# A linear-attention and mixture-of-experts kernel on one core: all steps put in another order by a planner with other prices for changes of the array's tiling

## The chip, the cores and the metric

The kernel runs on one core of one Trainium2 chip. The metric is the device time of one execution in microseconds, as the median of three runs. Engines are named as the profile names them: PE is TensorE (PEld its weight loads), DVE is VectorE, ACT is ScalarE, POOL is GpSimd, SP is the engine that issues most DMAs.

## What is computed

For 8 batches and 8 heads (sequence 576, head size 64), linear attention with a feature map, and then on its output a layer with 4 experts, each a causal softmax attention of its own, mixed by a gate that keeps the two best experts of a row:

```python
def phi(x):
    proj = np.einsum('bhsd,df->bhsf', x, w_phi)
    proj = proj - np.max(np.abs(proj), axis=-1, keepdims=True)
    return np.concatenate([np.exp(proj), np.exp(-proj)], axis=-1)
kv = np.einsum('bhsf,bhsd->bhfd', k_p, v)
num = np.einsum('bhsf,bhfd->bhsd', q_p, kv)
den = np.einsum('bhsf,bhf->bhs', q_p, z)[..., None] + 1e-06
x = num / den                          # per batch: 576 x 512
for e in range(4):
    q, k, v = x @ wq[e], x @ wk[e], x @ wv[e]
    a = softmax(causal(scale * q @ k.T))
    ye = a @ v @ wo[e]
    out += weight_of_gate(x @ w_gate, e) * ye
```

## The kernel before

Work is cut into steps. A pair is two heads of the first part (32 pairs in all, 4 to a batch); a half of a batch is two experts (16 halves in all). The steps on PE, with the line of the profile and the part of the 128x128 array that a matmul takes:

- **full array** (128 rows, 128 columns): L315, the helper `mm`, serves the projections of x to q and k (`ps_c<-xh,qk`), to v and the gate (`ps_c<-vg,xh`, five tiles a batch, called V steps here), the output projection (`ps_c<-yh,wo`, eight units a batch), and short warming matmuls on the tile `warm` that fill PE's waits at the start. L633 transposes.
- **64 rows**: L509, the feature projections of K and Q of a pair (`k_in`, `q_in` with `wf`), and L838, the scores, in four banks for each half.
- **32 columns**: L605 and L622 (kv and its sums of keys), L710 (denominators), L721 (numerators), L924 (gates), L1001 (the sums of the softmax), L1030 (attention times v).

So PE goes back and forth between three tilings of the array. A change of tiling is a point in PE's order where the next matmul takes another part of the array than the last.

All results land in eight PSUM tiles (`ps_c`), taken from one pool. A tile is free again when ACT or DVE has copied or used up what it holds: the two halves of Q's projection wait for copies on ACT (`evac_u`, L324), K's for DVE (`center`, L564 and L578), the denominators' and the softmax sums' for a chain DVE, ACT, DVE (`fractions`, L732, L326, L739, L742, L745) at the end of which the tile is released, the scores' for copies on ACT (`evac_s`).

After the scores of a half come the mask on POOL (L942), the running maximum over key blocks (`top`, L955, DVE), the maximum across partitions on POOL (L959, into the tile `max`), subtraction (L963, DVE), exponential (L326, ACT), two additions into `max` (L975, DVE), and the sums (L1001, PE). There is one `max` tile, so the L959 of a half has to wait until the L1001 of the half before has read it.

No order is written out by hand. Each stream of steps is a generator; the class `Plan` keeps an estimated clock for each engine, and at each turn looks for the steps that could start within `WINDOW` of the earliest and takes the one with the lowest position. Positions come from the tables `POS`, `POS1`, `BOFF` and `MOVE` (one number for each step), plus `OTHER` where a step would change the tiling; `SWITCH` is added to the start of such a step. What a matmul costs in the estimate stands in `mm`, `half_mm` and `scores`, and what a change costs in `run`:

```python
        if eng == 'PE' and tiling != self.tiling:
            cost += CHANGE[tiling == (128, 128)]
            self.tiling = tiling
```

with `CHANGE = (150.0, 190.0)`: 150 ns into 64 rows or 32 columns, 190 ns into the full array. The order in which the steps are taken is then fixed on each engine by `in_order`.

Of the kernel before, what the change touches and what calls it, by code (L numbers as in the profile page):

```python
# [16 lines left out]
B, H, S, D, F = 8, 8, 576, 64, 128  # L17
# [23 lines left out]
HOT = 22.62  # L41
SLOPE = (-27.1, -45.11, 31.37, 22.04, 0.2)
# [5 lines left out]
FLEX = (544, -30)  # L48
# [6 lines left out]
WINDOW = 53.0  # L55
SWITCH = 43.0
SLACK = 150.0
LATE = (1200.0, 500.0)
PHASE = 0.0
ZEROS = 34.47  # L60

MOVE = {
# [10 lines left out]
    'evu': (21.12, -4.06, 14.36, -18.44, 5.1, 15.91, 29.23, -7.85, 16.87, -12.86, 9.23, -24.49, -1.82, -0.22, -20.76, 24.81, 11.28, -7.35, 2.92, 2.45, 9.93, -6.72, -3.41, -34.68, -21.04, 1.48, -2.83, 22.44, -22.76, -6.25, 15.97, -11.69,),  # L73
    'ph0': (-8.14, 0.95, 0.11, -1.26, 2.32, -7.14, 14.26, 1.03, -4.68, 5.71, 17.28, -2.71, 7.54, -8.69, 8.12, 18.24, -7.03, 16.87, -6.18, -9.54, -25.96, 24.71, -7.89, 12.56, -1.56, 10.54, -2, -6.36, -29.4, -8.19, -24.29, 4.42,),
    'ph1': (0.98, -31.26, 7.61, 13.17, -13.03, -6.78, -4.19, 30.31, 1.24, 14.84, -16.58, -8.83, -2.18, 2.26, -24.69, 4.64, 4.19, -14.28, -5.42, 5.41, 8.16, -8.76, -6.61, 2.72, -6.37, 21.76, -7.17, -16.16, -0.85, 16.73, 11.84, -11.68,),
    'cen': (-18.81, 6.49, -10.84, 12.73, -20.02, 8.22, 2.67, -4.13, -37.26, -31.66, -22.98, -21.09, -1.99, 11.55, -10.57, 24.02, 3.96, -3.59, 2.44, 14.24, 5.39, 33.73, 12.84, 2.35, -5.61, -5.03, -22.36, 21.58, -8.41, -5.42, -15.78, 16.67,),
    'evd': (-0.53, -8.66, 7.47, -22, -18.99, -9.4, -18.15, 12.47, -19.84, 8.28, -2.9, -3.62, 17.77, 27.72, -5.5, -22.57, 11.69, -3.3, -11.95, -21.43, -1.49, 34.49, 13.92, 18.59, 3.14, 4.37, 4.81, 2.48, 26.02, 6.28, 12.39, -10.59,),
    'n1': (7.63, -9.91, 2.94, 8.61, 6.97, 3.71, 0.17, -10.61, -19.77, -1.78, -4.43, -30.48, -18.43, 0.14, 9.45, -11.23, -16.35, -18.78, 7.28, 10.47, 7.42, -28.12, 5.4, 14, -24.35, -5.88, -12.01, -7.61, 17.16, -5.33, -22.39, -11.91,),
    'div': (-24.16, 1.89, 13.29, 2.53, 0.65, -0.28, 8.21, -7.67, -3.37, 4.47, -12.51, 7.23, 1.58, -6.78, 5.93, 2.54, 10.1, -14.14, -5.17, -6.51, 26.08, -8.09, -24.63, 7.57, 4.12, 2.66, -35.81, -1.48, 11.92, -19.86, -16.37, -36.85,),
# [1077 lines left out]
```

## Time and profile before

| what | value |
|---|---|
| median of three runs | 617.29 us (616.87 to 617.4) |
| span of the profiled execution | 615.0 us |
| PE busy | 600.5 us, 98% of the span |
| DVE busy | 557.3 us, 91% |
| ACT busy | 432.0 us, 70% |
| POOL busy | 245.0 us, 40% |
| granted TensorE clock, mean | 0.997 |
| chain that ended last, by engine | PE 74%, DVE 15%, ACT 5%, DMA 2%, issue 2% |

The span runs from the first to the last instruction of the profiled execution, whose own time beyond its span was not recorded apart; the median lies 2.3 us above the span. Matmuls are pipelined and the ends of their rows are modelled, so a PE row's length is longer than the time until the next matmul starts, and a short wait of PE can lie under the row before it. In the chain of waits a PE piece is cut where the next begins, so its length is the time that the group took on the path.

### The profile page before, as it was taken

The numbers are of one execution on the slowest core, as the hardware profiler recorded it, in microseconds if no ns is written. First come the engines' busy times: TensorE is split into PE (matmuls) and PEld (weight loads), VectorE is DVE, ScalarE is ACT, GpSimd is POOL, SyncE is SP. The second block draws the span as 40 slices with busy tenths as digits, with TensorE's granted clock in tenths as the row PEclk, the third lists the DMA queues.
The fourth block names the chain that finished last, engine by engine and source line by source line (L and its number), as shares of the span: only waits on it lengthen the run. The fifth ranks groups of instructions, "written<-read, shape, count | busy, mean of one in ns | idle before, by whom it ended". The sixth has DMA issues, their size and how long they took to land.

```text
span 615.0 us, 19992 instructions
## 1 busy us (share of the span) xinstructions
PE 600.5 (98%) x8263; PEld 470.6 (77%) x8263; DVE 557.3 (91%) x1124; ACT 432.0 (70%) x1034; POOL 245.0 (40%) x167
## 2 busy tenths in 40 slices
PE   8999999999999999999999999999999999999987
PEld 7665788667796778768886868876889677878976
DVE  5899989999999999999899999999999998888793
ACT  4898786667687688677775885875796668556652
POOL 5635533453324644252333614418430706421420
PEclk9999999999999999999999999999999999999999
DMA  9553212253113431253214332144212311020022
GB/s 218 155 150 103 59 51 81 68 159 87 54 66 113 120 87 37 72 158 110 74 35 107 119 107 63 46 135 138 66 53 83 111 37 27 15 92 2 2 78 78
DMA packets 41610, 52.48 MB, mean 85 GB/s; under 512 B 21168, under 2 KB 24624, under 8 KB 41520
## 3 DMA queue, kind: packets, MB, share of 16 engines
q1 hardware_dynamic: 41200, 50.62, 28.5%
q8 instruction: 65, 1.06, 0.7%
q10 hardware_dynamic: 320, 0.59, 0.4%
q14 instruction: 25, 0.20, 0.1%
HBM read 36.64 MB, written 14.55 MB: 83 GB/s over the span
## 4 chain that ended last, share of the span: by engine, by line
PE 74%; DVE 15%; ACT 5%; DMA 2%; issue 2%; POOLq 1%; POOL 1%; SPq 0%; ACTq 0%; DVEq 0%
PE ps_c L315 29%; PE ps_c L509 9%; PE ps_c L605 9%; PE ps_c L721 7%; PE ps_c L1030 6%; PE ps_c L838 6%; PE ps_c L710 4%; DVE u L685 3%; DVE zs L546 2%; PE ps_c L622 2%; ACT ek L326 2%; PE ps_c L1001 1%; DVE s L963 1%; DVE ek L578 1%; DVE max L975 1%
## 5 line engine op out<-in xcount | busy, mean ns | idle before, releaser
L681 POOL PARTITION_ALL_REDUCE mx<-u x64 | 144.2, 2305 | 182.7 <-ACT u L324 165.9
L315 PE MATMUL ps_c<-xh,qk 128*128 128x320 f32 (+1 forms) x512 | 106.1, 298 | 0.0
L959 POOL PARTITION_ALL_REDUCE max<-top x16 | 59.9, 3745 | 101.5 <-DVE top L955 35.8
L315 PEld LDWEIGHTS ps_c<-xh,qk 128*128 128x128 f32 x512 | 82.7, 188 | 2.3 <-issue 0.7
L326 ACT ACTIVATE ek<-ek 128x1152 f32<-128x1152 f32 x64 | 75.0, 1171 | 5.7 <-DVE ek L578 5.0
L315 PE MATMUL ps_c<-xl,qk 128*128 128x256 f32 (+1 forms) x256 | 75.5, 295 | 0.0
L605 PE MATMUL ps_c<-ek,v_in 128*32 128x256 f32 x1280 | 75.4, 381 | 0.0
L963 DVE TENSOR_TENSOR s<-s,max 128x1152 f32<-128x1152 f32 (+4 forms) x80 | 68.3, 879 | 1.0 <-POOL max L959 1.0
L942 POOL TENSOR_SCALAR_AFFINE_SELECT s<-s 128x256 f32<-128x256 f32 (+1 forms) x80 | 41.5, 558 | 62.2 <-ACT s L324 61.9
L685 DVE TENSOR_TENSOR u<-u,mx 128x576 f32<-128x576 f32 x64 | 61.6, 975 | 3.9 <-POOL mx L681 3.9
L324 ACT COPY s<-ps_c 128x512 f32<-128x512 f32 (+4 forms) x152 | 52.7, 445 | 14.7 <-PE ps_c L838 14.4
L326 ACT ACTIVATE s<-s 128x1152 f32<-128x1152 f32 (+4 forms) x80 | 56.4, 740 | 8.6 <-DVE s L963 8.4
L605 PEld LDWEIGHTS ps_c<-ek,v_in 128*32 128x32 f32 x1280 | 39.7, 110 | 27.2 <-issue 1.3
L315 PE MATMUL ps_c<-vg,xh 128*128 128x260 f32 (+1 forms) x320 | 58.9, 286 | 0.3 <-ACT s L324 0.3
L564 DVE TENSOR_REDUCE pmax<-ps_c 128x4 f32<-128x512 f32 (+1 forms) x96 | 49.5, 539 | 8.1 <-PE ps_c L509 8.0
L315 PE MATMUL ps_c<-yh,wo 128*128 128x320 f32 (+1 forms) x256 | 53.1, 303 | 0.0
L326 ACT ACTIVATE mx<-u 128x576 f32<-128x576 f32 x64 | 43.9, 687 | 10.5 <-DVE u L685 10.4
L324 ACT COPY u<-ps_c 128x256 f32<-128x256 f32 (+1 forms) x127 | 41.6, 412 | 11.7 <-PE ps_c L509 11.4
L578 DVE TENSOR_TENSOR ek<-ps_c,pmax 128x512 f32<-128x512 f32 (+1 forms) x96 | 49.8, 537 | 0.0
L315 PEld LDWEIGHTS ps_c<-vg,xh 128*128 128x128 f32 (+1 forms) x320 | 47.4, 177 | 1.9 <-ACT s L324 0.8
L509 PEld LDWEIGHTS ps_c<-wf,k_in 64*128 64x128 f32 x576 | 41.9, 190 | 8.5 <-ACT u L324 3.0
L509 PE MATMUL ps_c<-wf,k_in 64*128 64x128 f32 x576 | 46.7, 283 | 1.5 <-ACT u L324 1.1
(124 smaller groups left out, 1399.4 us busy)
## 6 DMA issues: line engine op xcount, KB each, us to landing
v_in<-in_v_dram SPq DMA_DIRECT2D x32, 320.0 KB, 3.0
out_dram<-ot SPq DMA_DIRECT2D x32, 288.0 KB, 2.1
q_in<-in_qt_dram SPq DMA_DIRECT2D x60, 144.0 KB, 2.9
kvd<-kvt SPq DMA_DIRECT2D x104, 48.0 KB, 1.7
kv<-kvd SPq DMA_DIRECT2D x26, 192.0 KB, 2.6
k_in<-in_kt_dram SPq DMA_DIRECT2D x32, 144.0 KB, 2.8
k_in<-in_kt_dram SPq DMA_DIRECT2D x32, 128.0 KB, 2.8
q_in<-in_qt_dram ACTq DMA_DIRECT2D x4, 144.0 KB, 4.1
```

The lines of the kernel that those rows point to most:

```text
L315: nc.tensor.matmul(o, a, b, start=start, stop=stop, skip_group_check=True)
L324: nc.scalar.copy(o, i)
L326: nc.scalar.activation(o, i, func, **kw)
L509: nc.tensor.matmul(o, a, b, start=True, stop=True, skip_group_check=True)
L564: dve(n * 128, [mk], [pk]).tensor_reduce(out=m[:, us], in_=src, axis=AX.X, op=ALU.max, apply_absolute_value=True)
L578: dve(n * 128, [e1k], [pk, mk]).tensor_tensor(out=ek2[p % EKB][:, 1, us, :], in0=src, in1=m[:, us].unsqueeze(2).to_broadcast([128, n, 128] ...
L605: nc.tensor.matmul(o[g, 0:2], v_in[:, 4 * h + t if t < 4 else 8 + h, k:64:2], ek[:, :, u_, :].rearrange("p c (w f) -> p c w f", w=4), star ...
L681: nc.gpsimd.partition_all_reduce(M, U, 128, bass_isa.ReduceOp.absmax)
L685: (nc.gpsimd if st.eng == 'POOL' else nc.vector).tensor_tensor(out=U, in0=U, in1=M, op=ALU.subtract)
L721: nc.tensor.matmul(ps[g:g + 32, 0:n], kvi[:, 2 * k + h, 32 * c:32 * c + 32], P_[h][c][:, s0:s1], start=c == 0, stop=c == 1, skip_group_che ...
L959: nc.gpsimd.partition_all_reduce(big.rearrange("p e s -> p (e s)"), top.rearrange("p e s -> p (e s)"), 128, bass_isa.ReduceOp.max)
L963: dve(2 * (S - 128 * j), [('d', x, j)], [('max', z)], 1.11, True).tensor_tensor(out=block(s_, j, None, rows(j)), in0=block(s_, j, None, ro ...
```

## The change

Instructions, tiles, buffers and transfers stay. The planner's prices change: each of the six kinds of change of tiling (F full array, R 64 rows, C 32 columns) gets its own, the matmuls of 64 rows get dearer by 3 to 8%, those of the full array a little cheaper, and all numbers of the position tables are new. Of these tables two lines stand here for all:

```diff
-HOT = 22.62
-SLOPE = (-27.1, -45.11, 31.37, 22.04, 0.2)
+HOT = 17.96
+SLOPE = (-111.44, -251.27, 40.23, 60.34, 22.07)
-FLEX = (544, -30)
+FLEX = (544.69, -42.6)
-WINDOW = 53.0
-SWITCH = 43.0
-SLACK = 150.0
-LATE = (1200.0, 500.0)
+WINDOW = 54.35
+SWITCH = 52.31
+SLACK = 165.59
+LATE = (1273.05, 546.05)
...
-    'm1': (7.02, 3.31, 27, -26.54, -1.83, 9.53, -13, -0.23,),
+    'm1': (7.41, 35.39, 147.3, -15.84, -4.59, 231.04, -76.16, -16.72,),
...
-TRATE = 2.37
-CHANGE = (150.0, 190.0)
+TRATE = 2.4
+CHANGE = {'FR': 102.0, 'FC': 110.0, 'RF': 141.0, 'RC': 163.0, 'CF': 116.0, 'CR': 110.0}
-OTHER = 20.47
+OTHER = 26.82
+ROWS = (1.055, 1.083)
...
+def change_cost(a, b):
+    kind = ['C' if t[1] < 128 else 'R' if t[0] < 128 else 'F' for t in (a or (128, 128), b)]
+    return CHANGE.get(''.join(kind), 0.0)
...
-            cost += CHANGE[tiling == (128, 128)]
+            cost += change_cost(self.tiling, tiling)
...
-            cost = max(n / RATE, LDW) + 5
+            cost = max(0.4454 * n, LDW) + 4.3
...
-        plan.run('PE', 2 * alone * n / TRATE + 3, [w], r, tiling=(64, 128))
+        plan.run('PE', alone * ROWS[n == 128] * (2 * n / 2.37 + 3), [w], r, tiling=(64, 128))
```

Lines of the new kernel stand six further down (L509 is L515 there, L1001 is L1007).

Counted in the two orders, PE changes its tiling 169 times before and 212 times after. Stretches of the full array go from 46 to 58, those of 64 rows from 59 to 75, those of 32 columns from 64 to 79 (each counted where it is entered). The warming matmuls go from 117 to 132, all in the first part. On DVE 1126 instructions become 1122, on ACT 1040 become 1044, since each copy may go to either.

Three places. The first is on PE, in the third batch, after the denominators of a pair, its neighbour's kv and sums of keys (L605, L622 with `ek`, `zs`) come Q's projection (L509, two matmuls of 256 and two of 320 columns) and the numerators (L721). Before:

```order
L622 MATMUL ps_c_65<-ek_108,sel 32x4x32 x4
L509 MATMUL ps_c_68<-q_in_105,wf 128x256
L509 MATMUL ps_c_70<-q_in_105,wf 128x256
L509 MATMUL ps_c_64<-q_in_105,wf 128x320
L509 MATMUL ps_c_66<-q_in_105,wf 128x320
L721 MATMUL ps_c_68<-mx_137,kv_119 32x256 x2
L721 MATMUL ps_c_68<-mx_138,kv_119 32x256 x2
L721 MATMUL ps_c_68<-u_129,kv_119 32x256 x2
L721 MATMUL ps_c_68<-u_130,kv_119 32x256 x2
```

After:

```order
L628 MATMUL ps_c_69<-ek_108,sel 32x4x32 x4
L515 MATMUL ps_c_63<-q_in_105,wf 128x256
L515 MATMUL ps_c_64<-q_in_105,wf 128x256
L727 MATMUL ps_c_68<-mx_137,kv_119 32x256 x2
L727 MATMUL ps_c_68<-mx_138,kv_119 32x256 x2
L727 MATMUL ps_c_68<-u_129,kv_119 32x256 x2
L727 MATMUL ps_c_68<-u_130,kv_119 32x256 x2
L515 MATMUL ps_c_69<-q_in_105,wf 128x320
L515 MATMUL ps_c_63<-q_in_105,wf 128x320
```

The halves of Q's projection, which stood in one stretch, now have the first half of the numerators between them: two changes of tiling more. The tile that the numerators take (68) was Q's own a step earlier before, and is another one now.

The second place is on PE near the end, where the last V step (`vg`) is followed by the output projection of the last batch but one (`wo`) and the softmax sums of the last half but one (L1001). Before:

```order
L315 MATMUL ps_c_66<-vg,xl_146 64x260
L315 MATMUL ps_c_68<-yh_167,wo 128x256 x2
L315 MATMUL ps_c_68<-yl_168,wo 128x256
L315 MATMUL ps_c_68<-yh_169,wo 128x256 x2
L315 MATMUL ps_c_68<-yl_170,wo 128x256
L315 MATMUL ps_c_69<-yh_167,wo 128x320 x2
L315 MATMUL ps_c_69<-yl_168,wo 128x320
L315 MATMUL ps_c_69<-yh_169,wo 128x320 x2
L315 MATMUL ps_c_69<-yl_170,wo 128x320
L1001 MATMUL ps_c_70<-s_153,ones 32x64 x4
```

After:

```order
L321 MATMUL ps_c_64<-vg,xl_146 64x260
L1007 MATMUL ps_c_70<-s_153,ones 32x64 x4
L1007 MATMUL ps_c_70<-max_156,ones 32x224 x4
L1007 MATMUL ps_c_70<-s_153,ones 32x96 x4
L1007 MATMUL ps_c_70<-s_153,ones 32x32 x4
L321 MATMUL ps_c_69<-yh_167,wo 128x256 x2
L321 MATMUL ps_c_69<-yl_168,wo 128x256
L321 MATMUL ps_c_69<-yh_169,wo 128x256 x2
L321 MATMUL ps_c_69<-yl_170,wo 128x256
```

The sums stand ahead of the two output units that were ahead of them.

The third place is what these sums wait for, on DVE: the running maximum of the last half (`top`, L955) and the two additions of the half before (L975). Before:

```order
L955 TENSOR_TENSOR top_155<-s_154 128x2x448
L955 TENSOR_TENSOR top_155<-top_155,s_154 128x2x320
L955 TENSOR_TENSOR top_155<-top_155,s_154 128x2x192
L955 TENSOR_TENSOR top_155<-top_155,s_154 64x2x64
L963 TENSOR_TENSOR s_153<-s_153,max_156 64x2x64
L975 TENSOR_TENSOR max_156<-s_153 128x2x448
L975 TENSOR_TENSOR max_156<-max_156,s_153 128x2x320
```

After:

```order
L961 TENSOR_TENSOR top_155<-s_154 128x2x448
L981 TENSOR_TENSOR max_156<-s_153 128x2x448
L961 TENSOR_TENSOR top_155<-top_155,s_154 128x2x320
L981 TENSOR_TENSOR max_156<-max_156,s_153 128x2x320
L961 TENSOR_TENSOR top_155<-top_155,s_154 128x2x192
L961 TENSOR_TENSOR top_155<-top_155,s_154 64x2x64
```

The two additions have one maximum (of 320 columns) between them and two of the four behind them; the last subtraction (L963) went ahead of the whole row.

## Rows read from the trace of the kernel before

**Rows 1.** The page, part 1: busy time, share of the span and instructions of each engine.

```profile
span 615.0 us, 19992 instructions
PE 600.5 (98%) x8263; PEld 470.6 (77%) x8263; DVE 557.3 (91%) x1124; ACT 432.0 (70%) x1034; POOL 245.0 (40%) x167
```

**Rows 2.** Windows: start and end, length, each engine's busy time, clock, DMA.

```profile
50.00:580.00 530.00, 524.68 (x7187) 411.67 (x7184) 494.19 (x985) 375.71 (x913) 215.49 (x146) 1.00 0.27 78
```

**Rows 3.** PE's waits between 50 and 580 us, the longest four of seven: total, times, longest.

```profile
PE ps_c L838 <- DVE rb L745: 1.7, 2, 1.3
PE ps_c L509 <- ACT u L324: 1.1, 2, 0.6
PE ps_c L838 <- DVE xl L319: 1.0, 1, 1.0
PE ps_c L710 <- DMA kv<-kvd: 0.5, 1, 0.5
...
```

**Rows 4.** Chain of waits: start, length, what; 32 columns, after the same tiling and after another.

```profile
112.43 2.20 PE ps_c L605 x39
114.63 2.70 PE ps_c L1030 x56
...
356.56 2.66 PE ps_c L315 x18
359.22 2.84 PE ps_c L1030 x56
```

**Rows 5.** The same view for 64 rows: the 18 matmuls of a K step.

```profile
90.94 2.60 PE ps_c L838 x33
93.54 1.17 PE ps_c L509 x18
...
442.29 6.55 PE ps_c L315 x48
448.84 1.32 PE ps_c L509 x18
```

**Rows 6.** The same view for the full array: one V step alone, between scores.

```profile
313.03 1.63 PE ps_c L315 x12
```

**Rows 7.** Timeline of PE: the first matmuls of two V steps, twelve matmuls apart.

```profile
244.56 0.40 PE L315 MATMUL ps_c<-vg,xh 128*128 128x260 f32 x2
...
245.99 0.40 PE L315 MATMUL ps_c<-vg,xh 128*128 128x260 f32 x2
```

**Rows 8.** Timeline at 219 us: softmax sums, the release of their tile, the scores.

```profile
219.12 0.41 PE L1001 MATMUL ps_c<-s,ones 128*32 128x96 f32 x16
...
225.42 0.77 DVE L745 STREAM_TRANSPOSE rb<-ps_c 128x576 f32<-128x576 f32 x1
...
226.24 0.47 PE L838 MATMUL ps_c<-qh,kkh 64*128 64x448 f32 x1 [1.26 <-DVE rb L745]
```

**Rows 9.** Timeline near the end: maxima, additions, output units, sums, POOL's maximum.

```profile
582.63 1.80 DVE L955 TENSOR_TENSOR top<-top,s 128x640 f32<-128x640 f32 x3
...
584.74 1.09 DVE L975 TENSOR_TENSOR max<-s 128x896 f32<-128x896 f32 x1
...
585.85 0.40 PE L315 MATMUL ps_c<-yh,wo 128*128 128x256 f32 x2
...
585.94 0.82 DVE L975 TENSOR_TENSOR max<-max,s 128x640 f32<-128x640 f32 x1
...
587.54 0.32 PE L1001 MATMUL ps_c<-s,ones 128*32 128x64 f32 x8
...
588.37 3.58 POOL L959 PARTITION_ALL_REDUCE max<-top  x1 [6.72 <-PE ps_c L1001]
```

**Rows 10.** Timeline at the start: warming matmuls, DVE.

```profile
10.04 4.36 PE L315 MATMUL ps_c<-warm 128*128 128x128 bf16 x75
...
14.52 1.85 DVE L685 TENSOR_TENSOR u<-u,mx 128x576 f32<-128x576 f32 x1 [0.26 <-POOL mx L681]
...
16.30 1.27 DVE L564 TENSOR_REDUCE pmax<-ps_c 128x4 f32<-128x512 f32 x2
```

More of the change, by code (lines that the diff above doesn't have):

```diff
@@ L54 @@
 WINDOW_HAM = 3413.0
-WINDOW = 53.0
-SWITCH = 43.0
-SLACK = 150.0
-LATE = (1200.0, 500.0)
+WINDOW = 54.35
+SWITCH = 52.31
+SLACK = 165.59
+LATE = (1273.05, 546.05)
 PHASE = 0.0
-ZEROS = 34.47
+ZEROS = 28.2
 MOVE = {
[10 rows of a table removed]
[L73 to L79, printed above, removed]
[6 rows of a table removed]
-    'gate': (19.49, -11.43, -6.09, 0.85, 5.59, 17.09, 4.34, 6.95,),
-    't1': (6.21, -13.36, 7.09, -2.21, -6.96, -5.15, -13.11, -22.93,),
-    'out': (0.94, -2.47, -1.22, -1.17, -4.2, 1.36, 15.49, 6.05,),
-    'fin': (0, 0, 0, 0, 0, 0, 0, -0.18,),
-}
@@ L91 @@
-POS1 = {'wq': 24.27, 'wv': 48.25, 'wo': 6.32, 'n0': -29.41, 'n1': 1.65, 'k': -1.55, 'q': -17.83, 'v': 6.22, 'kv': -23.07, 'z': 0.35, 'cen': -7.3, 'evu': -37.47, 'ph0': 25.81, 'ph1': 20.93, 'div': 3.92, 'evd': -3.25, 'lk': -12.81, 'lq': 47.36}
-BOFF = (-5.07, 0.34, -2.66, -3.42, -4.38, 5.28, 25.26, 8.75)
-POS = {'fin': 20.11, 'p0': -6.7, 'p1': -66.09, 'v0': 14.93, 'gate': -16.07, 's0': 3.48, 's1': -24.31, 'm0': 14.77, 'm1': 13.89, 't0': -38.13, 't1': 12.5, 'out': 23.34}
[10 rows of a table added]
+    'evu': (208.22, -120.66, -21.82, -22.61, -16.71, -69.18, 165.88, -61.01, 237.38, 146.65, -167.82, -53.3, 248.63, 119.02, -277.18, 43.31, -235.6, -77, -194.35, 70.77, -305.4, 183.89, -3.86, -156.53, 2.84, -46.31, 80.54, 86.55, 16.54, -66.97, 137.96, -198.95,),
@@ new lines @@
+    'ph0': (27.44, 54.88, -96.31, 55.7, -0.74, -6.58, 46.74, -211.33, 112.41, 127.15, 144.36, -18.6, 144.21, -57.98, 337.59, 42.04, 145.16, 14.41, 49.26, -49.85, 81.72, 16.06, -54.75, 172.77, 103.18, -25.71, -128.25, 62.97, 51.69, -187.3, -12.88, -1.58,),
+    'ph1': (51.04, -185.15, 97.8, 311.74, 109.46, -9.8, -4.78, 80.65, 58.22, 151.09, -13.13, -179.25, 185.43, 39.28, -29.47, 95.76, -4.63, 63.95, -173.35, 98.94, -51.32, -22.26, 15.84, -84.66, 87.94, -17.29, 117.6, -39.93, -47.74, 178.93, -75.42, 295.48,),
@@ new lines @@
+    'cen': (89.75, 82.81, -83.16, -142.1, -70.22, 16.7, -65.11, -277.87, -16.42, -39.64, -97.91, -50.3, -103.81, 13.96, -50.77, 68.09, 6.96, 39.64, -82.26, -58.6, -60.54, -28.89, 25.71, -23.34, -212.23, 59.21, -126.89, 5.29, -246.55, -164.39, -59.85, -134.3,),
+    'evd': (-69.52, -188.56, 20.22, 20.85, 39.02, -6.93, -33.01, -46.09, -147.11, 184.47, -151, -106.86, -73.8, 71.54, -237.35, -13.59, -103.54, -31.34, -71.31, 15.7, -53.54, -20.66, 58.35, -23.95, 53.23, 24.85, 41.31, -54.42, 98.26, 118.15, -149.38, -120.33,),
@@ new lines @@
+    'n1': (75.59, -139.79, -149.7, -75.7, 23.15, -72.38, 117.13, 155.26, 15.86, 48.36, 24.57, 145.51, -33.45, -110.33, 28.21, 26.85, -18.75, -37.25, -448.32, -176.75, -25.95, -162.32, 118.17, 114.01, 33.01, -175.75, -75.24, -67.53, 38.17, -33.48, -510.45, 179.74,),
+    'div': (-89.49, -23.11, 60.23, -114.07, 158.85, 25.89, -137.24, -62.44, -304.95, -198.76, -23.11, 8.98, 39.87, -194.04, -258.93, -120.66, -251, -62.07, 14.2, -134.99, 27.84, -66.59, -78.15, -242.74, -52.76, 123.95, 113.22, -310.3, -194.65, 74.68, 12.61, -65.84,),
[6 rows of a table added]
@@ new lines @@
+    'gate': (25.45, -22.5, -40.62, -19.86, -55.33, -9.16, 4.09, -168.81,),
+    't1': (-53.98, -31.39, -136.77, 58.41, 19.35, 27.37, 166.59, -151.07,),
+    'out': (24.21, -15.56, -28.63, -23.3, 256.67, 354.4, -64.07, 135.51,),
+    'fin': (0, 0, 0, 0, 0, 0, 0, -66.52,),
+}
+POS1 = {'wq': 59.63, 'wv': 73.23, 'wo': 38.56, 'n0': -38.06, 'n1': -2.97, 'k': -4.98, 'q': -18.65, 'v': 35.6, 'kv': -27.42, 'z': -4.21, 'cen': -7.39, 'evu': -43.36, 'ph0': 33.11, 'ph1': 26.29, 'div': -2.32, 'evd': -1.5, 'lk': -29.43, 'lq': 88.64}
@@ L95 @@
+BOFF = (2.46, 7.77, -1.99, -6.4, -2.19, -13.35, 59.16, -31.41)
+POS = {'fin': 41.95, 'p0': -0.5, 'p1': -126.29, 'v0': 6.26, 'gate': -9.79, 's0': 6.86, 's1': -52.28, 'm0': 15.72, 'm1': 11.99, 't0': -38.64, 't1': 0.56, 'out': 13.69}
 NPAIRS = B * NP
-HEAD = 2.29
+HEAD = -9.35
 ADDS = (0, 2)
@@ L836, in scores @@
                             r = slice(64 * e, 64 * e + 64)
-                            plan.run('PE', max((c1 - c0) / RATE, LDW * m / 128) / 2 + 3, [pk], need, tiling=(64, 128))
+                            plan.run('PE', 1.031 * (max((c1 - c0) / RATE, LDW * m / 128) / 2 + 3), [pk], need, tiling=(64, 128))
                             nc.tensor.matmul(ps[:m, o:w], K[k_][r, 128 * j:128 * j + m], Q[q_][r, c0:c1],
```

30 rows, old and new, of the table MOVE are left out of this document.

## The prediction

> **What bounds the kernel now.** I read the busy times first [rows 1]. PE is busy for 600.5 of 615.0 us, DVE for 557.3. Cut to the long middle, 50 to 580 us, PE is busy for 524.7 of 530 us and DVE for 494.2 [rows 2]. So in the middle the sum of PE's work is the time, with 5.3 us of waits beside it; DVE has 35.8 us to spare there, though it runs close behind. The head and the tail are different. In the first 16 us PE fills its waits with warming matmuls [rows 10], and near the end one long chain through POOL, DVE and ACT sets the pace [rows 9].
>
> Then PE's waits in the middle [rows 3]. The four kinds shown make 4.3 us in six waits; three single short ones make it nine waits. Nearly all are for a PSUM tile that ACT or DVE has not released: scores waiting for the tile of the softmax sums (released by L745) or of a numerator (L319), projections of Q and K waiting for copies of u. These are the waits that another order can remove. Since the end of a PE row is modelled, a wait can be partly covered by the row before it. A row of these matmuls is about 0.4 us long while the next starts some 0.05 us later (2.70 us for 56 [rows 4]), so up to 0.35 us of each of the nine is hidden: 9 x 0.35 = 3.2. The waits of the middle are then worth 5.3 to 8.5 us. All sums below start from the profiled execution, 615.0 us of span, and add the 2.3 us by which the median of 617.3 lies above it.
>
> **Part 1, the changes of tiling.** The instructions are the same, so PE's own work changes by what stands between them. The price of a stretch in another tiling comes from pairs of equal groups in the chain of waits. A group of 56 attention matmuls takes 2.70 us after other matmuls of 32 columns and 2.84 us after the full array [rows 4]: 0.14 us for a stretch of 32 columns. A K step of 18 matmuls takes 1.17 us after scores, which have the same tiling, and 1.32 us after the full array [rows 5]: 0.15 us for a stretch of 64 rows. For the full array, a V step alone between scores takes 1.63 us until the scores go on [rows 6], while within a run of V steps twelve matmuls take 245.99 - 244.56 = 1.43 us [rows 7]: 0.20 us. The counts of the orders, after minus before, are 12 stretches of the full array, 16 of 64 rows, 15 of 32 columns. Sum: 12 x 0.20 + 16 x 0.15 + 15 x 0.14 = 2.4 + 2.4 + 2.1 = 6.9 us more on PE. It is on the path wherever PE is the bound, which by rows 2 is nearly everywhere in the middle. Where PE would have waited at that point in any case it costs nothing, so 6.9 is the upper end; the lower end is 0, if every new change stands in a wait. I take 6.9 and count what is won back apart, in part 3.
>
> The rows show 0.14 to 0.20 us for a stretch in another tiling. The Trainium skill, TensorEngine Tiling (Array Packing), Key Properties, states that changing the mode drains the engine, which speaks against this change and agrees with the sign of the rows. Its page TensorE: Matmul & The Clock Gate, Step-by-step: what each phase is for, gives a drain of about 128 cycles, at 2.4 GHz 53 ns as an estimate; by it the 43 changes would be 2.3 us and the sum below 614.7. The rows are three times that, so the sum goes by the rows.
>
> **Part 2, the end.** Near the end POOL waits 6.72 us for the softmax sums of the last half but one, and starts its last maximum at 588.37 [rows 9]; all that follows hangs on it. The sums start at 587.54, behind two output units that start at 585.85 on PE, and behind the two additions on DVE, the second of which ends at 586.76. After the change the two units stand behind the sums, which is worth up to 587.54 - 585.85 = 1.7 us on PE. The additions come earlier too: of the three maxima that take 1.80 us together only the largest stays ahead of the second addition, so that ends some 0.9 us earlier, near 585.9, when PE gets there. The last two maxima, some 0.9 us, end near 586.8, about when the sums have been read and POOL can start. What follows on POOL, DVE and ACT has the same instructions. So the end comes 1.7 us earlier at best; it comes none earlier if the exponentials that the additions need are late. I take 1.4, close to the better end, since ACT's exponentials of that half have been moved ahead of its copies of v.
>
> **Part 3, the waits for tiles.** A split like the one of Q's halves lets PE do something else while ACT copies. I counted in both orders how much PE work lies between the last matmul into a tile and the first of the next step that takes the tile, by group durations like those in rows 4 and 5. Places where a tile of Q is taken again within 1.2 us: 11 before, 6 after. Places where a tile of the softmax sums or a denominator is taken again within 5 us (its release took 226.2 - 219.5 = 6.7 us in rows 8): 6 before, 4 after. Together 17 and 10, a drop by 41%. One that I can name: the wait of 1.26 us of the scores at 226.24 [rows 8] was for the tile of the sums; after the change the last bank of these scores takes two other tiles, and the sums' tile is next taken by a projection 8 us later. 41% of the upper value of 8.5 us is 3.5 us, of the lower value of 5.3 us 2.2 us. I take 3.5, since the waits that this can remove are of the kind that rows 3 list. Bounds: nothing is removed, or all 8.5 us; new waits can also come, for one a V step that now takes the tile of a score bank 0.15 us of PE work behind that bank, with a copy of some 0.4 us and its handover still to come.
>
> **Part 4, the rest.** The 15 more warming matmuls cost 4.36 / 75 = 0.058 us each, 0.9 us, 12 of them before the second K step. That step starts behind them at 14.4, but DVE, which takes it up, is busy with L685 until 14.52 + 1.85 = 16.37 and begins on it only then [rows 10], and now has a cast and a subtraction of weights ahead of it as well. So I cost them at nothing; without that cover it is 0.9 us. DVE and ACT have the same work but for four copies that move from DVE to ACT. DMAs keep their size and number and are moved with their steps; the queues are not what PE waits for, with one wait of 0.5 us [rows 3].
>
> **Sum.** 617.3 + 6.9 - 1.4 - 3.5 = 619.3 us.
>
> **Rivals.** (a) The waits go almost entirely. The new order then pays 6.9 us for 8 us of waits and 1.4 us at the end: 617.3 + 6.9 - 1.4 - 8 = 614.8 us. For it speaks that the splits stand where PE waited for ACT and DVE, and that DVE has 35.8 us to spare in the middle. Against it: 10 of 17 narrow places are left. It is decided at 5.5 us won back, where the sum is even with before; below 616.1 it counts as faster.
> (b) The changes stand in waits. DVE follows PE so closely that a good part of the new changes falls where PE would have waited: some 2 us less than in the forecast, 617.3 us. Then the order is another and the time the same.
> (c) The splits miss. The waits stay at what they were, because DVE's queue and not the distance on PE sets the release, and the end is not shortened: 617.3 + 6.9 = 624.2 us at the outside, 622.5 with part of the gain at the end.
> (d) A change is cheaper than the pairs of rows say, by the third that the page's figure gives: 12 + 16 + 15 changes at 0.05 us are 2.2 us, and the sum is 614.6 us. The rows speak against it in all three tilings. I give it 0.03.
>
> **How the numbers follow.** A measurement of this kernel can tell about 0.2%, 1.2 us, from no change, so faster is below 616.1 and slower above 618.5. Forecast (618.5 to 622): 0.36. Rival (a): 0.26. Rival (b): 0.19. Rival (c): 0.16. Rival (d): 0.03. That is 0.29 faster, 0.19 the same and 0.52 slower. For the range I leave out about 0.1 at each side: the lower end of (a) and (d) below 613, and (c) above 624. The range of the forecast alone is 618.5 to 622.
>
> **What would show it right or wrong.** In the profile after, the chain of waits should again show groups of 56 attention matmuls with 2.70 and 2.84 us, and PE's busy time in the middle should be larger by the changes while the waits get fewer. The wait of the scores for L745 near 226 us should be gone. POOL's last maximum should begin earlier, counted from the last V step, by over 1 us. If PE's busy time grows by far less than 6.9 us, part 1 is wrong; if PE's waits in the middle do not fall, part 3; if POOL still waits for sums that start 1.7 us behind the last V step, part 2.

## The result, and the profile after

The changed kernel is slower: 626.48 us in the median of four runs beside 617.08 for the kernel before, a ratio of 1.0143 (95% interval 1.0106 to 1.0180). A second session, the first experiment below, gave 624.13 beside 616.21, a ratio of 1.0121 (1.0100 to 1.0142). The forecast was 619.3 us, in a range that ended at 624.0.

The profiled execution of the changed kernel was its quickest, 622.24 us with a span of 620.4. The lines of the changed file are six higher than before (L321 is the `mm` of L315, L515 the features of L509, and so on). First the page (busy times, chain of waits), then the window over the long middle with the same columns as [rows 2], and PE's waits in it, the longest seven of eleven (total, times, longest):

```profile
PE 603.5 (97%) x8278; PEld 464.8 (75%) x8278; DVE 567.0 (91%) x1120; ACT 430.7 (69%) x1038; POOL 247.4 (40%) x167
...
PE 82%; DVE 8%; ACT 5%; issue 2%; POOL 1%; DMA 1%; SPq 0%; DVEq 0%; POOLq 0%
```

```profile
50.00:580.00 530.00, 521.94 (x7085) 401.33 (x7078) 496.53 (x970) 373.23 (x909) 207.93 (x141) 1.00 0.27 78
```

```profile
PE ps_c L515 <- DVE xl L325: 1.9, 1, 1.9
PE ps_c L716 <- DVE yl L325: 1.7, 1, 1.7
PE ps_c L515 <- DVE u L342: 1.0, 1, 1.0
PE ps_c L321 <- ACT s L330: 0.7, 1, 0.7
PE ps_c L515 <- ACT s L330: 0.7, 1, 0.7
PE ps_c L844 <- DVE kvt L647: 0.5, 1, 0.5
PE ps_c L515 <- ACT u L330: 0.5, 1, 0.5
...
```

PE is busy for 3.0 us more than before [rows 1], not 6.9, and in the middle it stands idle for 530 - 521.94 = 8.1 us instead of 5.3 [rows 2]. The waits have not gone down. None of the four kinds of [rows 3] is on the list as it was, and others have come, the largest three for tiles that DVE has not released.

The places that the prediction names, by PE's and POOL's timeline: the first matmul of kv, the scores near 226 us, the last V step, the sums of half 14, POOL's last maximum, and PE's last matmul.

```profile
15.83 2.37 PE L611 MATMUL ps_c<-ek,v_in 128*32 128x256 f32 x40
...
226.21 1.27 PE L515 MATMUL ps_c<-wf,k_in 64*128 64x128 f32 x17 [0.65 <-ACT s L330]
...
593.20 0.28 PE L321 MATMUL ps_c<-vg,xl 128*64 128x260 f32 x1
593.41 0.32 PE L1007 MATMUL ps_c<-s,ones 128*32 128x64 f32 x8
...
594.24 3.64 POOL L965 PARTITION_ALL_REDUCE max<-top  x1 [4.29 <-DVE ge L903]
...
616.01 0.31 PE L321 MATMUL ps_c<-yl,wo 128*128 128x320 f32 x1
```

Before, the same rows stand at 16.08, 585.73, 587.54 [rows 9], 588.37 [rows 9] and 610.75. So the start is 0.25 us earlier; from the first kv matmul to the last V row it is 577.37 us instead of 569.65, 7.7 us more; and from there to the last matmul 22.81 instead of 25.02, 2.2 us less. That is 5.3 of the 5.4 us between the two spans. In these 577.37 and 569.65 us PE is busy for 568.50 and 563.88. So the 7.7 us are 3.1 us of idle time of PE (8.9 less 5.8) and 4.6 us in which PE works or changes its tiling: 0.11 us for each of the 43 new changes, if all of it is theirs. Groups of 56 attention matmuls again take 2.70 and 2.84 us in the chain of waits, as the prediction said.

The medians lie further apart than the two spans, since the executions of one kernel differ. The eight of the changed kernel, by mean granted clock: 623.36 us (1.000), 622.24 (0.999), 623.31 (0.998), 624.90 and 625.39 (0.997), 627.48 and 627.57 (0.994), 628.11 (0.993). The seven of the kernel before in the second session go from 615.42 (1.000) to 617.25 (0.997). Between the two executions at 1.000 (623.36 and 615.42) the difference is 7.9 us, so the clock accounts for little of the loss; most of it is there at full clock as well.

### The profile page after: what moved, and what is told of

It is laid out like the page before. It is cut to its first block, busy times and chain, and to the rows that moved or that the text cites. A ratio compares the mean times of both kernels' runs of the same rounds, so it can differ in the third digit from the quotient of the medians.

```text
span 620.4 us, 20035 instructions
## 1 busy us (share of the span) xinstructions
PE 603.5 (97%) x8278; PEld 464.8 (75%) x8278; DVE 567.0 (91%) x1120; ACT 430.7 (69%) x1038; POOL 247.4 (40%) x167
## 3 DMA queue, kind: packets, MB, share of 16 engines
q8 instruction: 65, 1.06, 0.7%
## 4 chain that ended last, share of the span: by engine, by line
PE 82%; DVE 8%; ACT 5%; issue 2%; POOL 1%; DMA 1%; SPq 0%; DVEq 0%; POOLq 0%
PE ps_c L321 31%; PE ps_c L515 10%; PE ps_c L611 10%; PE ps_c L727 9%; PE ps_c L1036 6%; PE ps_c L844 6%; PE ps_c L716 5%; PE ps_c L628 2%; PE ps_c L1007 2%; DVE s L969 2%; DVE u L691 1%; DVE max L981 1%; ACT u L330 1%; DMA k_in<-in_kt_dram 1%; ACT s L332 1%
## 5 line engine op out<-in xcount | busy, mean ns | idle before, releaser
L321 PE MATMUL ps_c<-xh,qk 128*128 128x320 f32 (+1 forms) x512 | 107.2, 300 | 0.0
L965 POOL PARTITION_ALL_REDUCE max<-top x16 | 58.3, 3646 | 113.2 <-DVE top L961 48.8
L948 POOL TENSOR_SCALAR_AFFINE_SELECT s<-s 128x256 f32<-128x256 f32 (+1 forms) x80 | 44.4, 582 | 113.9 <-ACT s L330 113.9
L321 PEld LDWEIGHTS ps_c<-xh,qk 128*128 128x128 f32 x512 | 82.9, 188 | 3.5 <-issue 1.1
L321 PE MATMUL ps_c<-xl,qk 128*128 128x256 f32 (+1 forms) x256 | 75.6, 295 | 0.0
L611 PE MATMUL ps_c<-ek,v_in 128*32 128x256 f32 x1280 | 75.4, 381 | 0.0
L691 DVE TENSOR_TENSOR u<-u,mx 128x576 f32<-128x576 f32 x64 | 64.3, 1012 | 2.2 <-POOL mx L687 2.1
L611 PEld LDWEIGHTS ps_c<-ek,v_in 128*32 128x32 f32 x1280 | 39.4, 110 | 28.4 <-issue 1.7
L321 PE MATMUL ps_c<-vg,xh 128*128 128x260 f32 (+1 forms) x320 | 58.8, 285 | 0.7 <-ACT s L330 0.7
L330 ACT COPY u<-ps_c 128x320 f32<-128x320 f32 (+1 forms) x122 | 41.9, 410 | 23.9 <-PE ps_c L515 23.0
L321 PE MATMUL ps_c<-yh,wo 128*128 128x256 f32 (+1 forms) x256 | 53.4, 303 | 0.0
L321 PEld LDWEIGHTS ps_c<-vg,xh 128*128 128x128 f32 (+1 forms) x320 | 47.4, 177 | 2.3 <-ACT s L330 1.4
L321 PEld LDWEIGHTS ps_c<-xl,qk 128*128 128x128 f32 x256 | 48.2, 188 | 0.0
L515 PEld LDWEIGHTS ps_c<-wf,k_in 64*128 64x128 f32 x576 | 39.0, 187 | 11.7 <-issue 2.9
```

The source lines that it names most:

```text
L321: nc.tensor.matmul(o, a, b, start=start, stop=stop, skip_group_check=True)
L330: nc.scalar.copy(o, i)
L515: nc.tensor.matmul(o, a, b, start=True, stop=True, skip_group_check=True)
L611: nc.tensor.matmul(o[g, 0:2], v_in[:, 4 * h + t if t < 4 else 8 + h, k:64:2], ek[:, :, u_, :].rearrange("p c (w f) -> p c w f", w=4), star ...
L691: (nc.gpsimd if st.eng == 'POOL' else nc.vector).tensor_tensor(out=U, in0=U, in1=M, op=ALU.subtract)
L965: nc.gpsimd.partition_all_reduce(big.rearrange("p e s -> p (e s)"), top.rearrange("p e s -> p (e s)"), 128, bass_isa.ReduceOp.max)
```

## Experiments

Three explanations of the 8 to 9 us were open: each change of tiling costs PE what part 1 said; the new order brings waits of its own; or the waits bring something more, such as the low clock. An expectation names the theories that its run was to tell apart, and "Theory 1" or "the second" behind it means those of the expectation just quoted.

**The same kernel once more.** No edit.

> The changed kernel once more, unaltered, to see what its spread of 622.2 to 628.1 us is made of. Its four runs had granted clocks of 0.999, 0.997, 0.994 and 0.993 in the order of their times 622.2, 625.4, 627.6 and 628.1. Theory 1 (the clock): in most executions PE's clock falls to the lower level somewhere in the middle, where PE now waits often, and the work after it runs slower; the times lie between 622 and 628 again, the slower ones with the lower clock, and a trace of a slower execution shows a stretch in the middle with a granted clock below 1.00 that the trace of the 622.2 us execution lacks. Theory 2 (waits that vary): the clock is a by-product of longer waits, for instance for transfers; then a slower execution has over 3 us more of PE's waits in stretches whose clock is 1.00.

Measured: 624.13 us, and this time the profile fell on an execution of 627.48 us (span 625.7). Windows of 2 us, of it and then of the execution of 622.24 us:

```profile
134.00:136.00 2.00, 0.14 (x6) 0.05 (x2) 2.00 (x7) 1.02 (x3) 2.00 (x2) 1.00 0.46 120
136.00:138.00 2.00, 2.00 (x16) 0.85 (x20) 2.00 (x5) 0.92 (x3) 0.78 (x1) 0.58 0.36 92
138.00:140.00 2.00, 2.00 (x28) 0.93 (x24) 1.96 (x4) 1.94 (x4) 0.00 (x0) 0.56 0.05 14
```

```profile
132.00:134.00 2.00, 0.36 (x8) 0.00 (x0) 2.00 (x6) 1.17 (x3) 2.00 (x2) 1.00 0.54 155
134.00:136.00 2.00, 1.78 (x28) 1.02 (x32) 2.00 (x6) 0.77 (x4) 1.05 (x1) 1.00 0.25 57
```

Both executions wait for 1.9 us at the same place, with the same Q step. In the slower one the granted clock then falls to the lower level for some 3.4 us, and PE does half as many matmuls per us. Laid over each other, matmul by matmul, the two traces differ at four places only: 1.7 us in the first 10 us of the trace (before the first kv matmul), 1.6 us here, 0.3 us near 209 us, and 1.6 us at the end, where the clock falls again; between these they run alike to 0.1 us. So the waits are the same in both, and Theory 1 holds: two of the four places are the low clock. In the first 10 us the windows show a clock of 1.00 in both, yet from 6 to 8 us PE does 14 matmuls in the slower execution and 21 in the other; why is open.

**The price of a change, measured by itself.** In the kernel before, in the middle of each of the 64 projections of Q and K, one small matmul more:

```
                           n == 0, n == 11, s1 - s0, pk, [xk[c][x_], ('qk', w_)])
+                        if n == 5:
+                            nc.tensor.matmul(ps[:, 448:452], warm[0:64, 0:128], warm[0:64, 0:4], start=True, stop=True, skip_group_check=True)
```

This is the one with 64 rows; the others have `warm[:, 0:128]` (full array) and, written to `ps[0:32, 448:452]`, `warm[:, 0:32]` (32 columns). The kernels with the full array and with 64 rows no longer compute what the reference does, so their times alone are used; all other work stays.

> The kernel before, with one more small matmul (4 columns, bf16, its result read by nobody) in the middle of each of the 64 projections of Q and K for the attention, in the same tiling of the full array. No change of tiling is added. Both theories: some 0.1 us each, 64 x 0.1 = 6 us more than before at most. It is the base for the next two.

> The same small matmul at the same 64 places, but with 64 rows, so that each place adds a stretch of 64 rows and a stretch of the full array: 128 changes of tiling. Theory 1 (a change costs what the pairs of rows said, 0.15 for a stretch of 64 rows and 0.20 for one of the full array): 64 x 0.35 = 22 us more than the run with the matmul in the full array. Theory 2 (a change costs a third of that, 0.05 us, and the time of the changed kernel comes from waits): 64 x 0.10 = 7 us more.

> The same at 32 columns: 64 stretches of 32 columns and 64 of the full array. Theory 1 (0.14 and 0.20 us): 64 x 0.34 = 22 us more than the run with the matmul in the full array. Theory 2 (0.05 us a change): 7 us more.

Measured: 621.26, 633.54 and 633.50 us (before 616.48). PE's timeline around one of the 64, in the full array and then with 64 rows (start and length in us, then the matmul's part of the array and its size):

```profile
347.83 0.28 PE L315 MATMUL ps_c<-xh,qk 128*128 128x256 f32 x1
347.96 0.18 PE L788 MATMUL ps_c<-warm 128*128 128x4 bf16 x1
348.00 0.37 PE L315 MATMUL ps_c<-xh,qk 128*128 128x256 f32 x1
```

```profile
354.37 0.28 PE L315 MATMUL ps_c<-xh,qk 128*128 128x256 f32 x1
354.58 0.17 PE L788 MATMUL ps_c<-warm 64*128 64x4 bf16 x1
354.69 0.39 PE L315 MATMUL ps_c<-xh,qk 128*128 128x256 f32 x1
```

The change into 64 rows delays the small matmul from 0.13 to 0.21 us after its forerunner, the change back delays the next from 0.04 to 0.11. In total 12.3 us for 128 changes, 0.096 us each, the same for 64 rows and 32 columns. That lies between the two theories, nearer to the second: for changes put in by themselves, the prices of part 1 were too high.

**The same inside stretches of 32 columns.** The small matmul stands ahead of the second numerator step of each pair (L721) and the second attention step of each half (L1030), 48 places.

> The kernel before, with one more small matmul (4 columns, 32 columns of the array, its result read by nobody) ahead of the second numerator matmuls of each pair and of the second attention step of each half, 48 places, all inside stretches of 32 columns. No change of tiling is added: the base for the next run. Some 0.1 us each, 5 us more than before at most.

> The same 48 places, the small matmul with 64 rows: 48 stretches of 64 rows and 48 of 32 columns more. Theory 1 (every kind of change costs the 0.10 us that the matmuls in the full array showed): 48 x 0.19 = 9 us more than the run with the matmul in 32 columns. Theory 2 (a change between these two tilings costs what the prediction took, 0.15 + 0.14): 48 x 0.29 = 14 us more. The splits of Q add changes of this kind.

Measured: 617.56 and 623.89 us (before 616.60): 6.3 us for 96 changes, 0.066 each, which is less than either theory. Between 60 and 590 us PE is idle for 5.0 us in the profile of the first and for 2.3 in that of the second, so 2.8 us of the added changes lie where PE waited before. Without that it is 9.1 us, 0.095 each, Theory 1. This is also what rival (b) spoke of, changes that stand in waits: nearly a third of the price was hidden there.

**The end alone.** The kernel before up to the last V steps, then what is left in the order of the changed kernel:

```
 ... V steps of batch 7 (L315) ...
+L1001 MATMUL ps_c<-s,ones / max,ones          (sums of half 14)
 L315 MATMUL ps_c<-yh,wo / yl,wo               (output units of batch 6)
-L1001 MATMUL ps_c<-s,ones / max,ones
```

> The kernel before with the order of the changed kernel from the last run of V steps on (the sums of half 14 ahead of the output units, the additions between the maxima, the output units of the last batch in the order of the changed kernel), and its own order up to there. Theory 1 (part 2 of the prediction is right): 1.4 us less than before, and the granted clock in the last 20 us decides another 1.6 us either way. Theory 2 (the end gained only because the clock stayed up in the one execution of the changed kernel that the profile shows): no less than before.

Measured: 614.42 us beside 616.48, a ratio of 0.9967 (0.9955 to 0.9979). Rows of PE and POOL as above:

```profile
585.69 0.28 PE L315 MATMUL ps_c<-vg,xl 128*64 128x260 f32 x1
585.90 0.32 PE L1001 MATMUL ps_c<-s,ones 128*32 128x64 f32 x8
...
586.73 3.64 POOL L959 PARTITION_ALL_REDUCE max<-top  x1 [1.30 <-DVE ge L897]
...
608.51 0.31 PE L315 MATMUL ps_c<-yl,wo 128*128 128x320 f32 x1
```

POOL starts 1.64 us earlier than before (588.37), and the last matmul comes 2.24 us earlier. The 0.6 us between the two fit the low clock in the profile of before, 0.50 at 600 to 602 us, which this execution did not have. Between executions at a mean clock of 1.000 (613.87 and 613.92 beside 615.51) the gain is 1.6 us. Theory 1.

**Half of one order, half of the other.** The order of one kernel up to 190 us, then what is left in the order of the other.

> The order of the kernel before up to 190 us, then all that is left in the order of the changed kernel: 206 stretches of one tiling instead of 170 (213 in the changed kernel), so nearly all of the new changes of tiling, but not the new waits near 130 us. Theory 1 (a change costs 0.10 us as the runs with the extra matmul say, the new waits of the first 200 us are 3 us, the end gives 2): 616.5 + 36 x 0.10 - 2.0 = 618 us, with no low clock in the middle. Theory 2 (a change costs 0.16 us as in the prediction, the waits have nothing to do with it): 616.5 + 36 x 0.16 - 2.0 = 620.3 us or more.

> The order of the changed kernel up to 190 us, then all that is left in the order of the kernel before, its end too: 177 stretches of one tiling, 7 more than before, but with the waits near 130 us. Theory 1 (the new waits are 3.1 us, and the low clock behind them 1.6 in most executions): 616.5 + 7 x 0.10 + 3.1 + (0 to 1.6) = 620.3 to 621.9 us. Theory 2 (the changes of tiling at 0.16 us are all of it): 616.5 + 7 x 0.16 = 617.6 us.

Measured: 619.64 us for before-then-after, 621.83 for after-then-before (before 616.81). The first has no low clock in any of its five executions (0.999 to 1.000). Against the kernel with the new end it loses 619.64 - 614.42 = 5.2 us, with 36 changes more. The window from 190 to 580 us of the two, before-then-after and then the new end (columns as in [rows 2]):

```profile
190.00:580.00 390.00, 386.87 (x5262) 297.42 (x5258) 363.52 (x710) 271.14 (x674) 156.10 (x104) 1.00 0.27 77
```

```profile
190.00:580.00 390.00, 386.92 (x5330) 305.32 (x5323) 361.79 (x723) 273.94 (x676) 156.03 (x107) 1.00 0.26 77
```

PE is idle for 3.1 us in both, so the loss is in the time in which it works and changes. By the medians it is 0.144 for each of the 36; in the two traces the way from the first kv matmul to the last V step differs by 5.0 us, 0.139 each. That lies between the two theories, nearer to the second. After-then-before costs 5.0 us more than before, with only 7 changes more; that is Theory 1. Its longest waits, and the 2 us windows around the longer of the two waits for `rb`, which ends at 231.09 us:

```profile
PE ps_c L844 <- DVE rb L751: 2.2, 2, 1.9
PE ps_c L515 <- DVE xl L325: 1.9, 1, 1.9
PE ps_c L515 <- DVE u L342: 1.0, 1, 1.0
PE ps_c L844 <- DVE xl L325: 1.0, 1, 1.0
```

```profile
228.00:230.00 2.00, 1.22 (x11) 0.73 (x8) 2.00 (x5) 1.44 (x8) 2.00 (x2) 1.00 0.70 183
230.00:232.00 2.00, 0.92 (x11) 0.86 (x11) 2.00 (x4) 1.33 (x3) 1.65 (x4) 1.00 0.64 173
232.00:234.00 2.00, 2.00 (x14) 1.97 (x13) 2.00 (x7) 1.47 (x5) 0.65 (x2) 0.73 0.13 45
234.00:236.00 2.00, 2.00 (x10) 2.00 (x9) 1.92 (x3) 1.66 (x3) 0.00 (x0) 0.50 0.00 0
```

That wait was 1.26 us before [rows 8] and is 1.86 here. So the two halves each have their own loss: the first 190 us of the changed order lose 5 us by waits and what follows on them, the rest some 5 us with no more waiting, by its changes as far as is known. With the 2.1 us of the end, 616.5 + 5.0 + 5.2 - 2.1 = 624.6, which lies between the two medians of the changed kernel.

**Repair, first try: another step on PE.**

```
 L727 MATMUL ps_c<-u,kv
+L611 MATMUL ps_c<-ek,v_in x20        (PE)
 L515 MATMUL ps_c<-q_in,wf x2
-L611 MATMUL ps_c<-ek,v_in x20
```

(the trace has two rows for each of these matmuls, 40 for L611), and on DVE the second copy of u (L342) directly behind the first.

> The changed kernel with two moves between 120 and 140 us: the step of 40 matmuls on the key features (L611) stands ahead of the two matmuls of Q that wait 1.87 us for the tile of a numerator, and on DVE the second copy of u stands directly behind the first, so that the K step at 128.85 us waits some 0.5 us less. All else stands as in the changed kernel. Theory 1 (the order makes these waits, and the granted clock falls to its lower level behind them in most executions): 1.9 + 0.5 us less, and the low stretch near 136 us, worth 1.6 us, is gone as well: 620 to 622 us in the median, and less spread. Theory 2 (these waits stand for work of DVE that is late in any order, and come back at the next step): no less than the changed kernel, 624.

Measured: 626.80 us, no gain; the one execution at a clock of 1.000 took 623.02, as the changed kernel does. PE's row:

```profile
136.33 4.05 PE L611 MATMUL ps_c<-ek,v_in 128*32 128x256 f32 x40 [2.26 <-DVE xl L325]
```

The step put ahead waits as well, for a tile that the next of DVE's splits L325 releases, and behind it the clock is low again (40 matmuls in 4.05 us, not 2.37). What is short there is not work for PE but released tiles.

**Second try: five instructions moved on DVE,** three near 130 us and two near 371 us.

> The changed kernel with the order of PE untouched and five instructions moved on DVE alone: near 130 us the first addition of half 0 (L981, not needed before 150 us) and a subtraction of a maximum (L691) stand behind the splits of the numerators (L325) instead of ahead of them, the second copy of u directly behind the first; near 371 us the same for one L981 and one L691 ahead of the split of an output (L325). Theory 1 (the tile that PE waits for is held by what stands ahead of its release on DVE): the waits of 1.87 and 1.66 us shrink by 1.8 and 1.2 us, that of 1.03 by 0.5, and the low clock near 136 us goes: 620 to 621 us. Theory 2 (DVE has more work there than time; whatever is moved back holds another tile): as in the run that moved the PE step, nothing, 624 to 626 us.

Measured: 625.65 us. DVE and POOL near 131 us, and DVE near 371:

```profile
131.51 1.59 DVE L691 TENSOR_TENSOR u<-u,mx 128x576 f32<-128x576 f32 x1
...
131.19 4.26 POOL L687 PARTITION_ALL_REDUCE mx<-u  x2 [6.33 <-ACT u L330]
...
373.18 0.49 DVE L325 TENSOR_TENSOR yl<-ps_c,yh 128x320 fp32r<-128x320 f32 x1 [1.06 <-ACT yh L330]
```

The subtraction L691 takes 0.72 us where the changed kernel has it, ahead of POOL's reduction. In its new place it runs beside POOL and takes 1.59. Q's wait is 2.38 us, longer than before the repair, so for this wait the run decided nothing. The wait of 1.03 us for the second copy of u did shrink, to 0.30. The wait of 1.66 us near 371 is 1.83 here, although an addition (L981) that stood ahead of its split L325 on DVE now stands behind it: DVE stands idle for 1.06 us ahead of the split, for a copy (`yh`) that ACT makes. So this wait was not set by DVE's order.

**Third try: the releasing instructions alone.** DVE's order near 131 us, no more:

```
 L745 RECIPROCAL
+L325 TENSOR_TENSOR xl (pair 7) x2
+L751 STREAM_TRANSPOSE xf
 L570 TENSOR_REDUCE pmax
-L751 STREAM_TRANSPOSE xf
 L570 TENSOR_REDUCE pmax
 L759 TENSOR_TENSOR x2
 L570 TENSOR_REDUCE pmax
-L325 TENSOR_TENSOR xl (pair 7) x2
```

> The changed kernel with the order of PE untouched and only DVE's order near 131 us changed: the two splits of the numerator of pair 7 (L325), whose inputs are there at 131.06 us, and the transpose L751 stand ahead of three maxima (L570) and two products (L759) instead of behind them. They release the two tiles that PE's Q step at 134.22 us waits 1.87 us for. Theory 1 (that wait is set by DVE's order): the release comes at about 132.5, the wait shrinks by 1.6 us: 1.6 us less than the changed kernel, and 1.6 more in the executions in which the low clock near 136 us goes: 621.5 to 623 us. Theory 2 (DVE has too much to do there): nothing, 624 to 626 us.

Measured: 623.43 us, the four executions between 622.37 and 623.60, all at a clock of 0.999 to 1.000. PE's Q step, and what DVE does next:

```profile
132.39 0.97 PE L515 MATMUL ps_c<-q_in,wf 64*128 64x256 f32 x4
...
138.22 3.27 DVE L552 TENSOR_TENSOR zs<-zs,ek 128x512 f32<-128x512 f32 x2
...
138.83 3.58 POOL L965 PARTITION_ALL_REDUCE max<-top  x1 [3.69 <-PE ps_c L1007]
...
141.54 0.43 PE L628 MATMUL ps_c<-zs,ones 128*32 128x128 f32 x8 [1.04 <-DVE zs L552]
```

The wait of 1.87 us is gone. So it was DVE's order that set this wait: Theory 1 on the cause. But the time comes back. Laid over the trace of the changed kernel, PE is 1.83 us ahead at the Q step, 1.2 ahead at the sums near 138 us (they wait for an addition of DVE's), and 0.06 ahead at 141.54: the two additions L552 take 3.27 us beside POOL's maximum, where the changed kernel has them ahead of it in 1.42. DVE has no idle time over 0.1 us from 127.4 to 143 us, which is the second theory's point. At full clock the repair brings nothing (622.37 to 623.60 beside 622.24 and 623.36); its median is lower because the clock stayed up in all four executions.

**The splits of Q taken back** at 8 places (the second half of Q directly behind the first, as far as tiles are free): 204 stretches instead of 213.

> The changed kernel with the second half of Q directly behind the first at 8 places where the change had put another step between (as far as tiles are free there): 204 stretches of one tiling instead of 213. Theory 1 (the splits hide nothing that counts, a change costs 0.10 to 0.12 us): 1 us less than the changed kernel, 623.5 us. Theory 2 (the splits let ACT copy while PE works, as part 3 of the prediction had it): each rejoined place brings a wait of some 0.5 us back, 8 x 0.5 - 1 = 3 us more, 627 us.

Measured: 634.37 us, 8 to 10 us more than the changed kernel. Its largest waits:

```profile
PE ps_c L515 <- ACT u L330: 2.4, 2, 2.0
PE ps_c L727 <- DVE xf L751: 2.2, 1, 2.2
...
```

Theory 2 in sign, and more than it said: PE is idle for 13.9 us between 50 and 580 us instead of 8.1. At one of the rejoined places Q waits 1.96 us for `u`, as part 3 supposed of an order without the splits, and the clock falls behind it. The run also gives other PSUM tiles to many later steps, so not all of its loss need come from the splits.

**A kernel faster than both.** The new end, and two moves on DVE in the order of before:

```
 L742 TENSOR_TENSOR ps_c<-ps_c,gc
+L745 STREAM_TRANSPOSE rb<-ps_c
 L685 TENSOR_TENSOR u<-u,mx
-L745 STREAM_TRANSPOSE rb<-ps_c
...
 L963 TENSOR_TENSOR s<-s,max
+L319 TENSOR_TENSOR xl<-ps_c,xh
 L963 TENSOR_TENSOR s<-s,max
-L319 TENSOR_TENSOR xl<-ps_c,xh
```

> The kernel before with the new end, and two instructions moved on DVE: L745 (the sums' tile that the scores wait for at 226.24 us) ahead of one subtraction L685, and a split L319 near 512 us ahead of a subtraction L963. Theory 1: the waits of 1.26 and 0.98 us shrink by 1.2 and 0.8 us: 614.4 - 2.0 = 612.4 us. Theory 2 (as above): 614.4 us.

Measured: 611.40 us beside 616.60, a ratio of 0.9912 (0.9897 to 0.9927). Its waits between 50 and 580 us, complete:

```profile
PE ps_c L509 <- ACT u L324: 1.1, 2, 0.6
PE ps_c L924 <- ACT u L324: 0.4, 1, 0.4
PE ps_c L838 <- DVE rb L745: 0.4, 1, 0.4
PE ps_c L315 <- ACT s L324: 0.4, 1, 0.4
PE ps_c L509 <- DVE ek L578: 0.2, 1, 0.2
```

The waits of 1.26 [rows 8] and 1.0 us [rows 3] are gone: Theory 1. Against the trace of the kernel with the new end, PE is 1.36 us further ahead behind the first move and 0.96 behind the second, and here both gains last to the end. That is 2.3 of the 3.0 us between the two medians; the executions also have a mean clock of 0.999 to 1.000, those of the new end of 0.996 to 1.000.

## Why the prediction was wrong

**Part 1, the changes: right mechanism, price too high.** The step that failed is the price of a stretch, 0.14 to 0.20 us from pairs of groups. Measured by themselves changes cost 0.096 us, in the changed order 0.11 (4.6 us for 43) to 0.14 (5.0 for 36), so that the term is 4.6 and not 6.9 (0.16 on average). The pairs were few, and each was read between steps that also hand tiles on; that this made the difference is argued, not shown. The Trainium skill, TensorEngine Tiling (Array Packing), Key Properties, has the sign right: a change of mode drains the engine. The estimate of 0.053 us from the Trainium skill, TensorE: Matmul & The Clock Gate, Step-by-step: what each phase is for, is a little over half of the 0.096 that the runs show.

**Part 2, the end: right.** POOL's start was to move by 1.4 to 1.7 us and moved by 1.64; the kernel with the new end alone gained 2.06 us in the median, 1.6 at equal clock.

**Part 3, the waits: the sign was wrong, and this is the error that decided.** Forecast -3.5 us, measured +3.1 from the first kv matmul to the last V row; between 190 and 580 us PE is idle for 3.1 us in either order, so the excess lies ahead of that. The step was to take the number of narrow places on PE's order, 17 and then 10, for the amount of waiting. The named wait for the tile of the sums at 226.24 [rows 8] did go, as forecast; a wait of 0.65 us for a copy of the scores stands at 226.21 in its place. And at one place at least a split hides what it was said to hide (the run that took them back). But the count looked at PE alone. The new waits of 1.87, 1.66 and 1.03 us are for tiles that DVE releases. What stands ahead of the release in DVE's order sets the first and the third: moving two L325 and one L751 took the first away, moving one L342 took 0.7 us off the third, and moving one L745 and one L319 took away the two that the kernel before had. The second hangs on a copy that ACT makes for DVE. And taking a wait away is not yet a gain: the 1.83 us won at the first were lost again within 10 us, since DVE had no idle time there. The bounds that the prediction set for this part had no end at which waits come in that were not there before, though it named a new wait as possible. The number to be counted was, for each tile, the work queued ahead of the instruction that frees it, on DVE and on what DVE waits for.

**Part 4, the rest: a term of 0.7 us was put at nothing.** The first kv matmul starts at 15.83 us, before at 16.08, in spite of 15 more warming matmuls, but between the profiles of the runs here it lies between 14.88 and 17.57 by the pace of the matmuls in the first 10 us, and these two differ in pace. The chain of waits has the block of warming matmuls ahead of the second K step (start and length), before and after:

```profile
10.10 4.29 PE ps_c L315 x75
...
9.18 4.96 PE ps_c L321 x87
```

The K step stands directly behind the block, and the first kv matmul follows 1.75 us after its start in both kernels. So the 12 more cost 0.67 us there, and DVE's L685 does not cover them; whether all of it reaches the end is not shown. The kernel faster than both, which has the old order up to there and the quick pace of the profile after, starts kv at 14.88.

**What the sum left out: the clock.** With measured terms it would have been 617.3 + 4.6 - 2.2 + 3.1 + 0.7 = 623.5 us, near the executions at a clock of 0.998 to 1.000 (622.24 to 623.36). The medians are 0.6 and 3.0 us above it. In the one slower execution that has a trace, the wait near 134 us is followed by a stretch at half clock, and the end has another; of the other executions only the mean clock is known. No part of the prediction priced a wait at more than its own length.

**The rivals.** Rival (c), splits that miss and waits that stay, gave 622.5 to 624.2 us and comes nearest, in part by luck: its reason, that DVE's queue sets the release, is the one that the runs show for most of the large waits, but the measured time is the sum of a smaller price and larger waits, with the end shortened in full. (a) and (b) supposed that waits go or cover the changes; for (b) the run with 64 rows inside stretches of 32 columns shows that this happens, though not in the changed order. (d) had a change cheaper than the sum did, which is so, but at 0.05 us it went too far, and it too let the waits shrink.

Left open: whether the changed order with all its DVE waits put right would beat the kernel before. At 0.096 us its 43 changes would still cost 4.1 us, of which the end gives back 2. Open too is why a change costs 0.11 to 0.14 us in the order and 0.096 by itself; a short wait that lies under the row before it counts as PE's work in the first two numbers.

## What to carry over

Count waits where the tile is released: list what stands ahead of the releasing instruction on its own engine and on the engine that feeds it, see whether that work is urgent, and whether the engine has idle time to catch up in. Two instructions moved on DVE gave 2 to 3 us in the order of before, three moved in the changed order gave nothing at equal clock, and an order of all steps that was finer on PE lost 8 to 9. Measure the price of an operation by adding many of it to the kernel, and a control that adds the same number of the kind that costs nothing, before multiplying a difference between two rows.

## What the runs showed of the hardware

The granted clock fell from 1.00 to 0.50, that is from 2.4 to 1.2 GHz, in the middle of the kernel after PE had been nearly idle: busy for 0.14 of 2 us, then some 3.4 us at the lower level, worth 1.6 us. The same wait left the clock at 1.00 in another execution of the same program. In after-then-before the wait of 1.86 us near 134 us left it at 1.00 and the one of 1.86 us at 231 us (above) was followed by 0.50; in the second try the wait of 2.38 us left it at 1.00 and the one of 1.83 us was followed by 0.50. So a wait of about 2 us can cost nearly twice its length, does so in some executions only, and its length alone does not tell which.

DVE slows beside POOL: L691 from 0.72 to 1.59 us beside a reduction across partitions, two L552 from 1.42 to 3.27. The Trainium skill, SBUF — State Buffer, SBUF: two separate sides, states that a DVE operation with two inputs in SBUF and an operation of GpSimd that reads it shut each other out of a shared pair of ports for a whole instruction; both rows are such pairs and agree in kind, though each of the DVE rows ends before POOL's does (L552 at 141.49, POOL's maximum at 142.41). So an instruction that is moved on DVE has the price of its new neighbour on POOL, not that of its old row.
